# Loading w_in in quarters, and new placement rules for early copies, query scalings and middle groups, in a fused recurrent-attention and feed-forward kernel

## The chip, the cores and the metric

The kernel runs on one core of a Trainium2 chip. The metric is device time in microseconds (us) of one launch. Lower is better. All five engines of the core are used: TensorE (PE) for matmuls, VectorE (DVE), ScalarE (ACT), GpSimd (POOL), and SyncE (SP), which only issues transfers.

## The reference

Inputs are q, k, v and f_logit of shape 4 x 8 x 768 x 48 (batch, heads, time, width), and two weight matrices. The first half is a recurrence per batch and head, the second a two-layer feed-forward network over the 3072 tokens:

```python
f = 1.0 / (1.0 + np.exp(-f_logit))
for t in range(S):
    state = f[:, :, t, :, None] * state + np.einsum('bhd,bhe->bhde', k[:, :, t], v[:, :, t])
    y[:, :, t] = np.einsum('bhd,bhde->bhe', q[:, :, t], state)
# x = y with the heads side by side: 3072 tokens x 384
h = x @ w_in                                   # 384 x 2048
g = 0.5 * h * (1.0 + erf(h * inv_sqrt2))       # exact gelu
out = g @ w_out                                # 2048 x 384
```

## The kernel before

Time is cut into 24 chunks of 128 tokens, six for each of the four batches. Per chunk, the kernel loads f_logit, k, q and v (four transfers of 192 KB on SP's queue, lines 322 and 326). Exponentials on ACT (E and L for the gate, then RG and GT, lines 336 to 356) turn the recurrence into matmuls within the chunk. DVE scales keys (KP, line 359) and queries (QP, line 363); POOL casts the values (VC, line 369). PE transposes keys and queries (Tk, Tq, line 406), DVE and ACT copy them out of PSUM (KB, QT, lines 412 and 415), PE multiplies them (A, line 425), DVE masks the product (AM, line 429), PE multiplies by the values (Y, lines 477 and 481), and four copies (X and three x, lines 490 and 493) write the result, transposed, into a tile xT. The state passes from chunk to chunk through S (line 441), R (line 456), T (POOL, line 458) and SB (POOL, line 464).

The feed-forward part works on groups of chunks, whose sizes are `SIZES`. F1 (line 515) multiplies xT by w_in into PSUM, so it needs the x of every chunk of its group. GE (gelu on ACT, line 519) writes gT. F2 (line 532) multiplies gT by w_out in four steps r, of which step r needs the quarter r of w_out. A copy O (line 538) and a store on SP's queue follow. The exponentials and the gelu live in two different activation tables of ACT, and a change between them is a table load (line 604).

The weights are loaded from POOL's queue, because they are cast from float32 to bfloat16 on the way. Before, w_in comes in two column halves W0 and W1 of six transfers each (load_win, line 295), and w_out in four parts O0 to O3 (line 299). `ORDER` says in which order chunks (c0, c1, ...) and weights are wanted.

The order of all work is laid down ahead by a small planner (class Plan). Each operation is added with an engine, an assumed duration, what it reads and writes, and a priority. The planner places operations one after the other by the earliest start it computes, and among equal starts by the lower priority number. An operation with `alt` may go to a second engine; a copy that would go to ACT as an alternative is charged `BIAS` for it. Transfers are one serial resource of their own for the planner: a chunk's load counts 1.05, a half of w_in 1.2 or 0.4 per transfer, a part of w_out 2.4, and each is visible 2.0 after its end. The time that POOL spends on issuing a weight transfer is not in the plan. Afterwards the instructions are emitted in order of planned start, those that load weights `EARLY` = 1.5 ahead of it (line 601). Each engine and each queue then runs its own in that order.

Lines 592 to 612 add one more rule. If a weight's transfer started less than 3.0 ahead of a chunk's f_logit load in the plan, that load waits on the chip until a weight planned to start at least 2.5 ahead of it has landed:

```python
elif o.name.startswith("ldf") and ws and ws[-1][1] > o.start - 3.0:
    early = [w for w in ws if w[1] < o.start - 2.5]
    if early:
        gates[o.name] = early[-1][0]
```

Rings limit how far an engine can run ahead: xT has three buffers, gT two, the gelu's PSUM tiles three, the attention's PSUM tiles three. Idle matmuls (line 587) fill PE's planned gaps in the first 26 us.

Of the kernel before, what the change touches and what calls it, by code (L numbers as in the profile page):

```python
# [2 lines left out]

# [50 lines left out]

LAT = {"PE": 0.28, "ACT": 0.12, "DVE": 0.12, "POOL": 0.15, "DMA": 2.0}
SWITCH = 1.28
JITTER = 2.0


class Op:  # L60
    __slots__ = ("eng", "dur", "fn", "bufs", "prio", "deps", "table", "start", "end", "vis", "seq", "name", "alt", "nb")


class Plan:


    def __init__(self, seed=0, bias=0.0):
        self.ops, self.w, self.r = [], {}, {}
        self.rnd, self.bias = random.Random(seed) if seed else None, bias

    def add(self, eng, dur, fn, rd=(), wr=(), bufs=(), prio=0.0, deps=(), table=None, name="", alt=None):
        o = Op()
        o.alt, o.nb = alt, 0.0
        o.eng, o.dur, o.fn, o.bufs, o.prio, o.table, o.name = eng, dur, fn, tuple(bufs), prio, table, name
        o.start = o.end = o.vis = None
        o.seq = len(self.ops)
        d = list(deps)
        for k in rd:
            d += self.w.get(k, [])
        for k in wr:  # L80
            d += self.w.get(k, []) + self.r.get(k, [])
        for k in rd:
            self.r.setdefault(k, []).append(o)
        for k in wr:
            self.w[k] = [o]
# [12 lines left out]

    def run(self):
        free = {e: 0.0 for e in LAT}  # L100
        if self.rnd:
            for o in self.ops:
                o.prio += self.rnd.uniform(-JITTER, JITTER)
        act = None
        wait = {id(o): len(o.deps) for o in self.ops}
        after = {}
        for o in self.ops:
            for d in o.deps:
                after.setdefault(id(d), []).append(o)
        left = [o for o in self.ops if not o.deps]  # L110
        placed = []
        while left:
            best, stay, cand = None, None, []
            for o in left:
                ok = True
                t0 = o.nb
                for b in o.bufs:
                    v = b.ready()
                    if v is None:
                        ok = False  # L120
                        break
                    t0 = max(t0, v)
                if not ok:
                    continue
                for eng, dur in ((o.eng, o.dur),) if not o.alt else ((o.eng, o.dur), o.alt):
                    t = max(t0, free[eng])
                    for d in o.deps:
                        v = d.end if d.eng == eng and eng != "DMA" else d.vis
                        t = v if v > t else t
                    if o.table and o.table == act and (stay is None or t < stay):  # L130
                        stay = t
                    cand.append((t, o, eng, dur))
            for t, o, eng, dur in cand:
                if o.table and act and o.table != act and stay is not None and stay < t + 2 * SWITCH:
                    continue
                key = (int((t + (self.bias if o.alt and eng == "ACT" else 0)) * 20 + 0.999), o.prio, o.seq, t + dur)
                if best is None or key < best[0]:
                    best = (key, t, o, eng, dur)
            if best is None:
# [24 lines left out]
def kernel(  # L164
# [50 lines left out]
    P = Plan(SEED, BIAS)  # L215

    def copy(dst, src):
        if P.cur.eng == "ACT":
# [72 lines left out]

    def load_win(kk, half, ch):
        p0, p1, r0 = ((0, 96, 96 * kk), (96, 128, 288 + 32 * kk))[half]
        cs = slice(ch * d_ff // 2, (ch + 1) * d_ff // 2)
        return nc.gpsimd.dma_start(out=win[p0:p1, kk, cs], in_=moe_w_in[r0:r0 + p1 - p0, cs])

    def load_wout(j):
# [31 lines left out]
    def stage1(g):  # L329
# [13 lines left out]
        for n in ns:  # L343
# [16 lines left out]
                x["kp"].t()[:, :, 0:D], x["kt"].t(), rg.t(), ALU.mult),  # L360
                rd=[("rg", n), ("kt", n)] + [f"kpz{i}" for i in range(NQ)], wr=[("kp", n)],
                bufs=[x["kp"], x["kt"], rg], prio=pr, name=f"KP{n}")
            P.add("DVE", 0.57, lambda x=x, gt=gt: nc.vector.tensor_tensor(  # L363
                x["qp"].t()[:, :, 0:D], x["qt"].t(), gt.t(), ALU.mult),
                rd=[("gt", n), ("qt", n)] + [f"qpz{i}" for i in range(NQ)], wr=[("qp", n)],
                bufs=[x["qp"], x["qt"], gt], prio=pr + 1, name=f"QP{n}")

            def cast(x=x):
                nc.gpsimd.tensor_copy(x["vp"].t().rearrange("p (h x) -> p h x", x=VB)[:, :, 0:D], x["vt"].t())  # L369
# [23 lines left out]
    def attn(n):  # L393
# [17 lines left out]
        for hh in range(2):  # L411
            P.add("DVE", 0.42, lambda hh=hh: copy(
                kb.t()[64 * hh:64 * hh + D, :, hh, :], tps[0].t()[64 * hh:64 * hh + D]),
                rd=[("tk", n), "kbz0", "kbz1"], wr=[("kb", n, hh)], bufs=[tps[0], kb], prio=pr + 4, name=f"KB{n}", alt=("ACT", 0.6) if KBALT and n < ALTN else None)
        P.add("ACT", 0.6, lambda: copy(qT.t(), tps[1].t()),
              rd=[("tq", n)], wr=[("qT", n)], bufs=[tps[1], qT], prio=pr + 4, name=f"QT{n}", alt=("DVE", 0.42) if n < ALTN else None)
        ams = []
        for half in range(2):
            ap_, am = r_as.new(), r_am.new()
# [68 lines left out]
        def cols():  # L488
            return slice(j * C, (j + 1) * C)
        P.add("DVE", 0.55, lambda: copy(xT.t()[0:96, :, cols()], yp.t()[0:96, 0:3 * C].rearrange("p (a t) -> p a t", t=C)),  # L490
              rd=[("yp", n, 0), ("yp", n, 1)], wr=[("x", n, 3)], bufs=[yp, xT], prio=pr + 2, name=f"X{n}", alt=("ACT", 0.51) if n < ALTN else None)
        for kk in range(KO):
            P.add("DVE", 0.29, lambda kk=kk: copy(
                xT.t()[96:128, kk, cols()], yp.t()[32 * kk:32 * kk + 32, 3 * C:4 * C]),
                rd=[("yp", n, 1)], wr=[("x", n, kk)], bufs=[yp, xT], prio=pr + 2, name=f"x{n}", alt=("ACT", 0.3) if n < ALTN else None)

    def ffn_group(g):
        s, t = SIZES[g], G[g]
# [9 lines left out]
        for u in range(FO // pk):  # L508
            hps = r_hp.new()

            def f1(u=u, hps=hps):
                for i in range(pk):
                    fo = u * pk + i
                    for kk in range(KO):
                        nc.tensor.matmul(hps.t()[:, i * tok:(i + 1) * tok], win[:, kk, fo * 128:(fo + 1) * 128],  # L515
                                         xT.t()[:, kk, 0:tok], start=(kk == 0), stop=(kk == KO - 1))
# [8 lines left out]
        for s_, r in ([(s_, r) for r in range(4) for s_ in range(s)] if g < RMAJOR  # L525
# [10 lines left out]
            if r < 3:  # L536
                continue
            P.add("ACT", 0.49, lambda op=op, osb=osb: copy(osb.t(), op.t()[:, 0:d_model]),
                  rd=[("o", n)], wr=[("os", n)], bufs=[op, osb], prio=pr - 1000, name=f"O{n}", alt=("DVE", 0.55) if n < ALTN else None)
# [105 lines left out]
```

## Time and profile before

| what | value |
|---|---|
| median of 3 runs | 206.8 us (206.2 to 206.98) |
| the profiled execution | 207.0 us |
| its span, first to last instruction | 205.2 us |
| PE busy | 188.4 us (92%) |
| ACT busy | 135.7 us (66%) |
| DVE busy | 124.2 us (60%) |
| POOL busy | 54.5 us (27%) |
| TensorE clock granted | 0.992 of full speed |

A busy PE in the table is not a PE at its peak: matmuls overlap, and each record covers the whole passage of one. The share of useful work has to be counted from the number of matmuls in a stretch.

### The profile page before, as it was taken

Reading aid. Unit: us, or ns where it says so; the run is one execution under the profiler, and the core shown is the slowest. Engines: PE = TensorE matmul, PEld = TensorE weight load, DVE = VectorE, ACT = ScalarE, POOL = GpSimd, SP = SyncE. Lnnn points to the kernel's source line nnn. Section 1 sums busy time; section 2 is a strip of 40 time slices with the busy share of each in tenths; the row PEclk is TensorE's granted clock in tenths of the full one; section 3 lists DMA queues with packets and bytes.
Section 4 is the critical chain, followed back from the end, with each engine's and each line's share of the span. In section 5 each row is a group of like instructions: output and inputs, shape, how many; then the busy total and the mean of one; then the engine's idle time right before and its main releaser. Section 6 shows DMA issues by size and latency. Waiting matters only on the chain.

```text
span 205.2 us, 4574 instructions
## 1 busy us (share of the span) xinstructions
PE 188.4 (92%) x1735; PEld 127.7 (62%) x1746; DVE 124.2 (60%) x270; ACT 135.7 (66%) x247; POOL 54.5 (27%) x117
## 2 busy tenths in 40 slices
PE   6798769988889987997999999999999999999993
PEld 5797734556568666865665668655676655644551
DVE  6598750019793899999999579964189862000000
ACT  4445349954588677986977973887977773169510
POOL 7238990004023134422344032030032200000000
PEclk9799999999999999999999999999999999999999
DMA  7999999999999999998999999300121000220022
GB/s 125 189 171 161 183 168 159 191 181 239 205 206 186 188 227 192 167 203 192 202 189 175 190 202 221 86 0 2 42 77 38 3 0 0 80 77 0 0 77 77
DMA packets 106388, 27.02 MB, mean 132 GB/s; under 512 B 100480, under 2 KB 105600, under 8 KB 106368
## 3 DMA queue, kind: packets, MB, share of 16 engines
q1 hardware_dynamic: 103296, 23.60, 64.4%
q0 software_dynamic: 3072, 3.15, 10.1%
q8 instruction: 13, 0.21, 0.5%
q14 instruction: 7, 0.06, 0.1%
HBM read 25.17 MB, written 4.72 MB: 146 GB/s over the span
## 4 chain that ended last, share of the span: by engine, by line
PE 66%; DVE 10%; SPq 8%; DMA 7%; issue 4%; ACT 2%; POOL 1%; DVEq 0%; ACTq 0%; POOLq 0%
PE hps L532 26%; PE hps L515 24%; SPq L326 7%; PE aps L477 4%; DMA fl<-in_f_logit_dram 4%; PE tp L406 4%; PE aps L425 3%; DVE am L429 3%; DVE xT L221 2%; DMA vt<-in_v_dram 2%; PE aps L481 2%; PE aps L441 1%; DVE qp L363 1%; DMA out_dram<-osb 1%; DVE kp L359 1%
## 5 line engine op out<-in xcount | busy, mean ns | idle before, releaser
L515 PE MATMUL hps<-xT,win 128*128 128x512 bf16 (+1 forms) x325 | 68.0, 347 | 2.8 <-DVE xT L221 2.1
L532 PE MATMUL hps<-wout,gT 128*128 128x384 bf16 x384 | 68.2, 326 | 0.0
L519 ACT ACTIVATE gT<-hps 128x512 bf16<-128x512 f32 x96 | 56.4, 597 | 12.5 <-PE hps L515 8.3
L532 PEld LDWEIGHTS <-gT 128*128 128x128 bf16 x384 | 36.4, 98 | 21.9
L515 PEld LDWEIGHTS <-win 128*128 128x128 bf16 x336 | 31.5, 98 | 26.3 <-issue 3.5
L221 DVE CAST xT<-aps 96x384 bf16<-96x384 f32 (+1 forms) x92 | 32.7, 355 | 9.2 <-PE aps L481 6.0
L429 DVE TENSOR_TENSOR am<-aps,mask 128x512 bf16<-128x512 f32 x48 | 31.0, 685 | 6.8 <-PE aps L425 6.4
L369 POOL CAST vp<-vt 128x384 bf16<-128x384 f32 x24 | 12.7, 530 | 62.7 <-DMA vt<-in_v_dram 37.3
L477 PE MATMUL aps<-am,vp 128*128 128x128 bf16 x192 | 19.9, 219 | 3.0 <-DVE am L429 2.6
L458 POOL TENSOR_TENSOR tn<-rr,gl 128x384 f32<-128x384 f32 x16 | 13.2, 827 | 30.5 <-DVE rr L456 21.9
L359 DVE TENSOR_TENSOR kp<-kt,rg 128x384 bf16<-128x384 f32 x24 | 14.6, 609 | 11.0 <-ACT rg L356 10.7
L219 ACT ACTIVATE osb<-hps 128x384 f32<-128x384 f32 x18 | 8.8, 490 | 18.6 <-PE hps L532 18.4
L477 PEld LDWEIGHTS <-vp 128*128 128x128 bf16 x192 | 15.5, 98 | 8.5 <-issue 3.5
L464 POOL CAST sb<-tn 48x192 bf16<-48x192 f32 x40 | 16.0, 399 | 12.3 <-PE aps L477 3.9
L221 DVE COPY kb<-tp 48x512 bf16<-48x512 bf16 x42 | 17.5, 418 | 0.6
L336 ACT ACTIVATE fl<-fl 128x384 f32<-128x384 f32 (+2 forms) x15 | 10.7, 714 | 10.5 <-DMA fl<-in_f_logit_dram 10.4
L356 ACT ACTIVATE rg<-aps 128x384 f32<-128x384 f32 x24 | 11.8, 491 | 7.2 <-PE aps L349 6.1
L604 ACT ACT_TABLE_LOAD x12 | 15.4, 1283 | 0.9 <-PEq L629 0.7
L587 PE MATMUL hps<-trin 128*128 128x128 bf16 x170 | 14.0, 242 | 1.4 <-POOL trin L231 1.4
L425 PE MATMUL aps<-qT,kb 128*128 128x128 bf16 x192 | 15.0, 221 | 0.3 <-DVE qT L221 0.3
L481 PE MATMUL aps<-qT,sb 128*128 128x128 bf16 x80 | 15.1, 219 | 0.0
L219 ACT ACTIVATE qT<-tp 128x512 bf16<-128x512 bf16 x18 | 10.7, 596 | 6.5 <-PE tp L406 6.4
(42 smaller groups left out, 174.0 us busy)
## 6 DMA issues: line engine op xcount, KB each, us to landing
fl<-in_f_logit_dram SPq DMA_DIRECT2D x24, 192.0 KB, 4.5
kt<-in_k_dram SPq DMA_DIRECT2D x24, 192.0 KB, 4.6
qt<-in_q_dram SPq DMA_DIRECT2D x24, 192.0 KB, 4.5
vt<-in_v_dram SPq DMA_DIRECT2D x24, 192.0 KB, 4.5
out_dram<-osb SPq DMA_DIRECT2D x24, 192.0 KB, 1.9
wout<-in_moe_w_out_dram POOLq DMA_DIRECT2D x4, 384.0 KB, 7.9
win<-in_moe_w_in_dram POOLq DMA_DIRECT2D x6, 192.0 KB, 4.8
win<-in_moe_w_in_dram POOLq DMA_DIRECT2D x6, 64.0 KB, 4.3
```

Of the source, the lines that this page charges most:

```text
L219: nc.scalar.activation(dst, src, AF.Copy)
L221: nc.vector.tensor_copy(dst, src)
L359: P.add("DVE", 0.57, lambda x=x, rg=rg: nc.vector.tensor_tensor(x["kp"].t()[:, :, 0:D], x["kt"].t(), rg.t(), ALU.mult), rd=[("rg", n), ("k ...
L425: nc.tensor.matmul(ap_.t()[:, i * C:(i + 1) * C], kb.t()[:, p, hh, :], qT.t()[:, p, :], start=True, stop=True)
L429: P.add("DVE", 0.69, lambda ap_=ap_, am=am: nc.vector.tensor_tensor(am.t(), ap_.t().rearrange("p (h t) -> p h t", t=C), mask.unsqueeze(1). ...
L464: nc.gpsimd.tensor_copy(sb.t()[64 * hh:64 * hh + D, :, D * hh:D * hh + D], tn.t()[64 * hh:64 * hh + D, :, D * hh:D * hh + D])
L477: nc.tensor.matmul(yp.t()[:, p * C:(p + 1) * C], vwin(vp.t(), 2 * p + hh), ams[half].t()[:, 2 * (p % 2) + hh, :], start=(hh == 0), stop=(h ...
L481: nc.tensor.matmul(yp.t()[:, p * C:(p + 1) * C], osb.t()[:, p, :], qT.t()[:, p, :], start=False, stop=True)
L515: nc.tensor.matmul(hps.t()[:, i * tok:(i + 1) * tok], win[:, kk, fo * 128:(fo + 1) * 128], xT.t()[:, kk, 0:tok], start=(kk == 0), stop=(kk ...
L519: acts.append(P.add("ACT", 0.6, lambda u=u, hps=hps: nc.scalar.activation(view()[:, u * pk:(u + 1) * pk, :].rearrange("p a b -> p (a b)"), ...
L532: nc.tensor.matmul(op.t()[:, 0:d_model], view()[:, fo, s_ * C:(s_ + 1) * C], wout[:, fo, :], start=(fo == 0), stop=(fo == FO - 1))
L604: nc.scalar.preload_act_table_set("natural_log_exp_and_others" if table == "exp" else "gelu_and_others")
```

## The change

- w_in is loaded in four column quarters (`NW = 4`), six transfers each, so 24 instead of 12. F1 waits for the quarter that it reads.
- `ORDER` is now c0 to c3, then W0 to W3, then c4, then O0 to O3. Before, O3 came ahead of W0, O1 ahead of c4, and O0 and O2 behind it.
- `SIZES` goes from 4,2,2,4,4,4,4 to 4,2,2,1,2,1,4,4,4. The exponentials' batches end in 4,4 instead of 4,2,1,1.
- Alternatives: QP of the first six chunks may go to POOL (`QALTN = 6`). KB may no longer go to ACT (`KBALT = 0`). QT, X, x and O may change engine for four chunks instead of six (`ALTN`). The charge for leaving the home engine is 0.4 instead of 0.8 and holds in every direction. The planner, which is run twice, remembers the home engine.
- Fixed offsets are added to the priorities by kind of operation (`PRI`). The unused random offsets are removed.
- `LOCK` is 4 instead of 12: rules that tie an exponentials' batch to a gelu hold from chunk 4 on.

```diff
-        o.eng, o.dur, o.fn, o.bufs, o.prio, o.table, o.name = eng, dur, fn, tuple(bufs), prio, table, name
+        o.eng, o.dur, o.fn, o.bufs, o.prio, o.table, o.name = eng, dur, fn, tuple(bufs), prio + self.pri.get(name.rstrip("0123456789."), 0), table, name
...
-                for eng, dur in ((o.eng, o.dur),) if not o.alt else ((o.eng, o.dur), o.alt):
+                for eng, dur in ((o.home, o.dur),) + (o.alt or ()):
...
-                key = (int((t + (self.bias if o.alt and eng == "ACT" else 0)) * 20 + 0.999), o.prio, o.seq, t + dur)
+                key = (int((t + (self.bias if eng != o.home else 0)) * 20 + 0.999), o.prio, o.seq, t + dur)
...
-    SIZES = [4, 2, 2, 4, 4, 4, 4]
-    ORDER = ['c0', 'c1', 'c2', 'c3', 'O3', 'W0', 'W1', 'O1', 'c4', 'O0', 'O2']
+    SIZES = [4, 2, 2, 1, 2, 1, 4, 4, 4]
+    ORDER = ['c0', 'c1', 'c2', 'c3', 'W0', 'W1', 'W2', 'W3', 'c4', 'O0', 'O1', 'O2', 'O3']
     EARLY = 1.5
+    NW = 4
...
-    LOCK = 12
-    KBALT = 1
-    ALTN = 6
-    BIAS = 0.8
-    SEED = 0
+    LOCK = 4
+    KBALT = 0
+    ALTN = 4
+    BIAS = 0.4
+    PRI = {'VC': 5, 'E': 1, 'KP': 10, 'X': -2, 'QT': 20, 'x': -1, 'Y': 2, 'SB': -1, 'A': 1, 'S': 2}
+    QALTN = 6
...
-    BATCH = [1, 1, 1, 1, 1, 1, 2, 2, 2, 2, 2, 4, 2, 1, 1]
+    BATCH = [1, 1, 1, 1, 1, 1, 2, 2, 2, 2, 2, 4, 4]
...
+    def eng():
+        return nc.vector if P.cur.eng == "DVE" else nc.gpsimd
...
-        cs = slice(ch * d_ff // 2, (ch + 1) * d_ff // 2)
+        cs = slice(ch * d_ff // NW, (ch + 1) * d_ff // NW)
...
-            P.add("DVE", 0.57, lambda x=x, gt=gt: nc.vector.tensor_tensor(
+            P.add("DVE", 0.57, lambda x=x, gt=gt: eng().tensor_tensor(
                 x["qp"].t()[:, :, 0:D], x["qt"].t(), gt.t(), ALU.mult),
...
-                bufs=[x["qp"], x["qt"], gt], prio=pr + 1, name=f"QP{n}")
+                bufs=[x["qp"], x["qt"], gt], prio=pr + 1, name=f"QP{n}",
+                  alt=(("POOL", 0.9),) if n < QALTN else None)
...
-            P.add("PE", 0.645 + 0.0025 * (3 * pk - 3), f1, rd=[("x", n, i) for n in ns for i in range(4)] + [f"win{u * pk // 8}"],
+            P.add("PE", 0.645 + 0.0025 * (3 * pk - 3), f1, rd=[("x", n, i) for n in ns for i in range(4)] + [f"win{u * pk * NW // FO}"],
...
-            P.w[f"win{ch}"] = [P.add("DMA", (1.2, 0.4)[half], lambda kk=kk, half=half, ch=ch: load_win(kk, half, ch),
+            P.w[f"win{ch}"] = [P.add("DMA", (2.4, 0.8)[half] / NW, lambda kk=kk, half=half, ch=ch: load_win(kk, half, ch),
```

More of the change, by code (lines that the diff above doesn't have):

```diff
@@ L1 @@
-import random
 from contextlib import ExitStack
@@ L56, with __init__ @@
 SWITCH = 1.28
-JITTER = 2.0
 class Op:
-    __slots__ = ("eng", "dur", "fn", "bufs", "prio", "deps", "table", "start", "end", "vis", "seq", "name", "alt", "nb")
+    __slots__ = ("eng", "dur", "fn", "bufs", "prio", "deps", "table", "start", "end", "vis", "seq", "name", "alt", "nb", "home")
 class Plan:
-    def __init__(self, seed=0, bias=0.0):
+    def __init__(self, pri, bias):
         self.ops, self.w, self.r = [], {}, {}
-        self.rnd, self.bias = random.Random(seed) if seed else None, bias
+        self.pri, self.bias = pri, bias
     def add(self, eng, dur, fn, rd=(), wr=(), bufs=(), prio=0.0, deps=(), table=None, name="", alt=None):
         o = Op()
-        o.alt, o.nb = alt, 0.0
-        o.eng, o.dur, o.fn, o.bufs, o.prio, o.table, o.name = eng, dur, fn, tuple(bufs), prio, table, name
+        o.alt, o.nb, o.home = alt, 0.0, eng
+        o.eng, o.dur, o.fn, o.bufs, o.prio, o.table, o.name = eng, dur, fn, tuple(bufs), prio + self.pri.get(name.rstrip("0123456789."), 0), table, name
         o.start = o.end = o.vis = None
@@ L100, in run @@
         free = {e: 0.0 for e in LAT}
-        if self.rnd:
-            for o in self.ops:
-                o.prio += self.rnd.uniform(-JITTER, JITTER)
         act = None
@@ L213 @@
     tpp = ctx.enter_context(tc.tile_pool(name="tpp", bufs=2, space=PSUM))
-    P = Plan(SEED, BIAS)
+    P = Plan(PRI, BIAS)
+    def eng():
+        return nc.vector if P.cur.eng == "DVE" else nc.gpsimd
     def copy(dst, src):
@@ L413, in attn @@
                 kb.t()[64 * hh:64 * hh + D, :, hh, :], tps[0].t()[64 * hh:64 * hh + D]),
-                rd=[("tk", n), "kbz0", "kbz1"], wr=[("kb", n, hh)], bufs=[tps[0], kb], prio=pr + 4, name=f"KB{n}", alt=("ACT", 0.6) if KBALT and n < ALTN else None)
+                rd=[("tk", n), "kbz0", "kbz1"], wr=[("kb", n, hh)], bufs=[tps[0], kb], prio=pr + 4, name=f"KB{n}", alt=(("ACT", 0.6),) if KBALT and n < ALTN else None)
         P.add("ACT", 0.6, lambda: copy(qT.t(), tps[1].t()),
-              rd=[("tq", n)], wr=[("qT", n)], bufs=[tps[1], qT], prio=pr + 4, name=f"QT{n}", alt=("DVE", 0.42) if n < ALTN else None)
+              rd=[("tq", n)], wr=[("qT", n)], bufs=[tps[1], qT], prio=pr + 4, name=f"QT{n}", alt=(("DVE", 0.42),) if n < ALTN else None)
         ams = []
@@ L490, in attn @@
         P.add("DVE", 0.55, lambda: copy(xT.t()[0:96, :, cols()], yp.t()[0:96, 0:3 * C].rearrange("p (a t) -> p a t", t=C)),
-              rd=[("yp", n, 0), ("yp", n, 1)], wr=[("x", n, 3)], bufs=[yp, xT], prio=pr + 2, name=f"X{n}", alt=("ACT", 0.51) if n < ALTN else None)
+              rd=[("yp", n, 0), ("yp", n, 1)], wr=[("x", n, 3)], bufs=[yp, xT], prio=pr + 2, name=f"X{n}", alt=(("ACT", 0.51),) if n < ALTN else None)
         for kk in range(KO):
@@ L494, in attn @@
                 xT.t()[96:128, kk, cols()], yp.t()[32 * kk:32 * kk + 32, 3 * C:4 * C]),
-                rd=[("yp", n, 1)], wr=[("x", n, kk)], bufs=[yp, xT], prio=pr + 2, name=f"x{n}", alt=("ACT", 0.3) if n < ALTN else None)
+                rd=[("yp", n, 1)], wr=[("x", n, kk)], bufs=[yp, xT], prio=pr + 2, name=f"x{n}", alt=(("ACT", 0.3),) if n < ALTN else None)
     def ffn_group(g):
@@ L538, in ffn_group @@
             P.add("ACT", 0.49, lambda op=op, osb=osb: copy(osb.t(), op.t()[:, 0:d_model]),
-                  rd=[("o", n)], wr=[("os", n)], bufs=[op, osb], prio=pr - 1000, name=f"O{n}", alt=("DVE", 0.55) if n < ALTN else None)
+                  rd=[("o", n)], wr=[("os", n)], bufs=[op, osb], prio=pr - 1000, name=f"O{n}", alt=(("DVE", 0.55),) if n < ALTN else None)
             P.add("DMA", 0.6, lambda n=n, osb=osb: nc.sync.dma_start(out=out[n * C:(n + 1) * C, :], in_=osb.t()),
```

## The prediction

> **What bounds the kernel now.** I first asked where PE, busy for 92% of the span, does no useful work. The counts of matmuls by line, priced at the pace of unbroken runs in the chain (43 of 512 columns in 9.44, 64 of w_out in 10.41, eight of 128 in 0.45), give 7.1 us of useful work in 0 to 29, 10.7 of 11 in 29 to 40, 13.6 of 18 in 40 to 58, 31.7 of 39 in 58 to 97, 30.9 of 33 in 97 to 130. So about 22 us go before F1 starts, 4.4 in 40 to 58, 7.3 in 58 to 97; from 97 on a floor of some 6% (2.1 of 33) is lost. The same 6% of 39 is 2.5, so 58 to 97 holds 4.8 that could be had back.
>
> The second view is the page's rows of 40 slices (5.1 us each), with two of its groups:
>
> ```profile
> DVE  6598750019793899999999579964189862000000
> POOL 7238990004023134422344032030032200000000
> DMA  7999999999999999998999999300121000220022
> L369 POOL CAST vp<-vt 128x384 bf16<-128x384 f32 x24 | 12.7, 530 | 62.7 <-DMA vt<-in_v_dram 37.3
> L604 ACT ACT_TABLE_LOAD x12 | 15.4, 1283 | 0.9 <-PEq L629 0.7
> ```
>
> POOL, nearly idle elsewhere, is full in slices 4 and 5, transfers are full up to about 128, and DVE is full again from 70 to 112. Third, POOL in order of time (start, us, idle before):
>
> ```profile
> 17.16 0.93 POOL L299 DMA_DIRECT2D wout<-in_moe_w_out_dram  x1
> 18.09 0.55 POOL L295 DMA_DIRECT2D win<-in_moe_w_in_dram  x1
> 18.66 0.83 POOL L458 TENSOR_TENSOR tn<-rr,gl 128x384 f32<-128x384 f32 x1
> ...
> 21.62 0.71 POOL L369 CAST vp<-vt 128x384 bf16<-128x384 f32 x1
> 22.28 1.99 POOL L295 DMA_DIRECT2D win<-in_moe_w_in_dram  x4
> ...
> 28.27 2.29 POOL L299 DMA_DIRECT2D wout<-in_moe_w_out_dram  x3
> 43.69 0.50 POOL L369 CAST vp<-vt 128x384 bf16<-128x384 f32 x1 [13.13 <-DMA vt<-in_v_dram]
> 48.13 0.51 POOL L369 CAST vp<-vt 128x384 bf16<-128x384 f32 x1 [3.93 <-DMA vt<-in_v_dram]
> ```
>
> Issuing one w_in transfer takes POOL 0.5 whatever its size; POOL works without a gap from 17.2 to 30.6. All three remaining w_out parts are out before VC4, which waits for chunk 4's values until 43.69. Fourth, SP's own waits, SP in order of time, and PE where F1 of the groups 0 and 1 starts:
>
> ```profile
> SPq L322 <- DMA win<-in_moe_w_in_dram: 15.4, 1, 15.4
> ```
> ```profile
> 32.10 0.37 SPq L322 DMA_DIRECT2D fl<-in_f_logit_dram  x1
> ```
> ```profile
> 29.02 10.52 PE L515 MATMUL hps<-xT,win 128*128 128x512 bf16 x47 [1.26 <-DVE xT L221]
> 39.38 3.41 PE L532 MATMUL hps<-wout,gT 128*128 128x384 bf16 x20
> 57.66 1.24 PE L515 MATMUL hps<-xT,win 128*128 128x256 bf16 x6 [0.47 <-DVE xT L221]
> ```
>
> The one gated load is chunk 4's f_logit: 15.4 of wait for w_in, and everything behind it on SP waits too. F1 of group 0 waits for x of chunk 3, not for w_in; F1 of group 1 waits for x of chunk 5.
>
> **What the Trainium skill says.** "DMA: Bandwidth & Descriptors", "Anatomy of one DMA — SWDGE (gpsimd) path": a wait before a transfer is held by the issuing sequencer, not by the DMA engines. The trace agrees: SP stood 15.4 and issued nothing. "GPSIMD Engine Reference", "4.1 Engine selection": an elementwise operation of two inputs is about twice as slow on GpSimd. Here 827 ns (line 458) against 552 to 593 on DVE, 1.4 to 1.5 times. "SBUF — State Buffer", "SBUF: two separate sides": DVE with two SBUF inputs and a GpSimd operation that reads SBUF exclude each other. QP3 at 21.27 took 0.70 beside VC3's 0.71 (usually 0.55 and 0.50), which agrees. "ScalarE: Activation LUTs", "What ACT_TABLE_LOAD costs": 1283 ns and a drain of 1380. The trace has the 1283, but the next activation follows the load at 40.20 after 0.01; I use 1.28.
>
> **The change, part by part.**
>
> *w_in in quarters.* Twelve more issues on POOL: 12 x 0.51 = 6.1 us. They fall where POOL is full. Up to VC2 nothing changes, so the 18th issue (the end of W2) comes at 17.1 + 18 x 0.51 + T2 0.8 + SB2 1.0 + VC3 0.7 + T3 0.8 + SB3 0.8 = 30.4, with one QP on POOL (0.83) 31.2, less 1.6 if T3 and SB3 fall behind it. Landing takes 4.3 to 4.8 (transfers' rows of the page, 192 and 64 KB): 34 to 36; I take 35. The last w_in issue is at 34, its landing at 38. F1 of group 0 has 10.5 us of work; it may start 0 to 4 earlier (DVE gets relief, below), but its last quarter cannot start before 38 and takes 2.6: end at 40.6, against 39.5. So the quarters gain nothing for F1. The half-as-long pieces may slow the transfers: not at all, or at worst to the rate of a chunk's loads, which are of the same 768 KB in far smaller pieces and came 4.2 apart (casts at 7.17 and 11.37). POOL's pace (six issues 3.1, with the work between them 4.3) covers even that.
>
> *The new order.* The planner's own costs tell the order, not the time. c0 to c3 end at 16 x 1.05 = 16.8, W3 at 16.8 + 9.6 = 26.4, c4 at 30.6, O0 starts there, O1 at 33.0, O2 at 35.4, O3 at 37.8. VC4 is ready at 30.6 + 2.0 = 32.6, on a POOL that is free in the plan. O2 is emitted at 35.4 - 1.5 = 33.9, O3 at 36.3. So VC4 now stands ahead of O2 and O3 on POOL, and they cannot be issued until the values of chunk 4 have landed. Before, VC4 was ready at 37.4 and the last O emitted at 36.3. The gates change as well: c4's load waits for the last transfer of W2 (planned 23.8, under 26.4 - 2.5), c5's load (planned 40.2) for O2 (35.4).
>
> That is a chain: W2 lands at 35; c4's four loads take from 6.3 (0.74 to the cast at 7.17, an uncrowded queue) to 11.5 (32.10 to 43.69 here); 8 is taken, so 43. VC4 0.5; O2 issued 43.5 to 44.3; it lands 5 to 7.9 later (7.9 is the page's median for w_out in a crowd; by then little else moves), 49.5, O3 at 51. Then c5's loads, 6.3: 56, against 48.1. F2 of chunk 0 runs its steps r = 0 and 1 near 42 to 44 and stands until 49.5 for r = 2. What stands behind it on PE are its own 14 steps (14 x 0.65 = 9.1) and A4, Y4. x5 followed the cast VC5 of 48.13 by 9.5; from 56, and with 7.6 to 9.5, it comes at 63.6 to 65.5. F1 of group 1 then starts near 64 instead of 57.7: **+6.4**, with ends of +2 (W2 at 34, c4 in 6.3, O2 in 5, x5 in 7.6: 59.5) and +10.
>
> *Placement of early copies, QP on POOL.* DVE sheds up to 6 x 0.59 of QP, six QT at 0.42 (the charge now falls on QT's move to DVE) and takes back six KB at 0.42 from ACT: 3.5 us less, all in chunks 0 to 5. This shortens the way to x3, worth 0 to 4 us alone, but F1's end is held by W3 as shown: 0 taken. A QP3 that sits on POOL among the w_in issues would come at about 23 instead of 21.3, which is also covered until 38. In chunks 4 and 5 the shorter DVE work is the lower end of 7.6 used above.
>
> *Smaller middle groups.* PE's columns are the same: 128-column matmuls run at 0.056 each (eight in 0.45), 256-column ones at 0.109 (30 in 3.27), so no group size costs PE anything that the trace shows. Gelu stays at 96 activations. What they bring: F1 need not wait for four, or two, chunks' x. F1 of chunks 8 to 11 started at 97.3 only when x11 was there; now F1 of chunk 8 can fill PE before. Of the 4.8 to be had in 58 to 97 I take 3; the bounds are 0 and 4.8. **-3**.
>
> *Table loads.* Twelve now, one pair per alternation. Two more groups can cost up to four more, 4 x 1.28 = 5.1 us of ACT. ACT is busy for 31.0 of 39 us in 58 to 97, so half might reach PE. The planner avoids a switch where work of the same table is near, so 0 is taken; 0 to 2.6.
>
> *Offsets, LOCK, the last batches.* The new tie of chunks 6 and 7's exponentials to group 0's last gelu holds at a time (41) when those chunks are not loaded; the last batch of four instead of 2,1,1 lies at 130 and later, where PE has a backlog: 0, with -1 to +1.
>
> Sum on the profiled execution: span 205.2 + 6.4 - 3 = 208.6, and 1.8 around it (207.0 - 205.2): 210.4. The median of the runs lies 0.2 below that execution: 210.2. Part of the delay may be absorbed, since PE had stood again at 74 to 80 for chunks 6 and 7 whatever happened before; I take 0.7 for it: **209.5**.
>
> **The rivals.** 0.5% of 206.8, about 1.0 us, is what a measurement can tell from no change.
>
> (a) *The transfers' chain is covered and the middle wins.* If c4 is back by 41 and O2 lands by 46, F1 of group 1 is late by 2 or less, and DVE's 3.5 us are felt in x5. Then -4.8 and +2 or 0: 202 to 204, best guess 203.5. For it: the stalls in 58 to 97 are real, and DVE was full there. Against it: POOL's issue time is measured and the order is arithmetic. It decides at a delay of about 4 in F1 of group 1. Chance 0.28.
>
> (b) *They cancel*: late by 4 to 5, middle back by 4 to 5, 206 to 207.8. Chance 0.15. It includes that the quarters do nothing since x3 holds F1.
>
> (c) *ACT becomes the bound in the middle*: four more table loads, no gain from the groups, the full delay: 205.2 + 6.4 + 2.6 + 1.6 = 215.8; with half of each 212.5. Against it: ACT idles a fifth there. Chance 0.09.
>
> The forecast itself, 207.8 to 212, has 0.48.
>
> **How the numbers follow.** Slower is the forecast and (c), 0.57; same (b), 0.15; faster (a), 0.28. The likeliest is 209.5, its own range 207.8 to 212. The range that leaves out two tenths runs from 203.3 (about half of (a) below it) to 212.5 (the worse half of (c) above it).
>
> **What would show it.** F1 of group 0 ends near 40.6 with a stand before its last quarter. On POOL two w_out issues come after VC4, at 43 to 45. SP waits for wout at c5. DMA has a hole in slices 9 and 10. F2 stands 4 or more us near 45, and F1 of group 1 starts at 62 or later. After that PE loses under 5 in the 39 us that follow. Wrong: O2 issued before VC4; W2 landed by 32; F1 of group 1 before 60; more than 14 table loads.

## The result, and the profile after

| | before | changed |
|---|---|---|
| median | 206.73 us | 212.63 us (211.57 to 213.34) |
| ratio, 95% interval | | 1.0285 (1.0231 to 1.0339) |
| profiled execution, its span | 207.0, 205.2 | 212.11, 210.1 |
| F1 of group 0: start, end | 29.0, 39.5 | 32.0, 47.1 |
| start of F1 of group 1 | 57.7 | 62.6 |
| from there to the end | 147.5 | 147.5 |
| table loads | 12 | 16 |

The kernel became slower, as forecast, but by 5.9 us instead of 2.8, and its time lies 0.13 above the stated range, which is less than the spread of its own runs. The two rows ahead of the last already divide it: all of the 4.9 us of span are lost before F1 of group 1 starts, and nothing is won afterwards. Of the kernels timed further below, one (e_halves_both) was profiled in a slower execution at a lower clock than most of its runs, so its profile is read only up to the start of F1 of group 1.

The rows of the page that answer to those shown of before (40 slices of 5.25 us; PEclk is the granted TensorE clock in tenths):

```profile
DVE  6589450002958286879989998947789771000000
POOL 7259994030603404312303543213041200000000
PEclk9999669699999997999999999999999999999999
DMA  7999789969999989999999999900111000220022
...
L605 ACT ACT_TABLE_LOAD x16 | 20.5, 1283 | 1.0 <-PEq L630 0.7
```

POOL is now full from 15.8 to 31.5, in three slices instead of two. The transfers have holes in the same stretch and from 42.0 to 47.3. The clock falls to 0.6 from 21.0 to 31.5 and again from 36.8 to 42.0, where the kernel before had full speed. POOL in order of time (start, us, idle before):

```profile
16.65 2.74 POOL L295 DMA_DIRECT2D win<-in_moe_w_in_dram  x5
19.39 0.86 POOL L459 TENSOR_TENSOR tn<-rr,gl 128x384 f32<-128x384 f32 x1
...
23.35 0.50 POOL L370 CAST vp<-vt 128x384 bf16<-128x384 f32 x1
23.80 4.44 POOL L295 DMA_DIRECT2D win<-in_moe_w_in_dram  x9
...
32.16 1.55 POOL L299 DMA_DIRECT2D wout<-in_moe_w_out_dram  x2
42.45 0.50 POOL L370 CAST vp<-vt 128x384 bf16<-128x384 f32 x1 [8.74 <-DMA vt<-in_v_dram]
42.90 1.49 POOL L299 DMA_DIRECT2D wout<-in_moe_w_out_dram  x2
```

This is the block that was forecast: O2 and O3 leave only after the cast of chunk 4 at 42.45. But the cast of chunk 3, at 21.62 before, is also late, at 23.35. SP's own waits show the two gates, for w_in at c4 and now for w_out at c5 too:

```profile
SPq L322 <- DMA win<-in_moe_w_in_dram: 13.7, 1, 13.7
SPq L322 <- DMA wout<-in_moe_w_out_dram: 13.7, 1, 13.7
```

PE where F1 of the groups 0 and 1 and the third step of F2 start, and ACT ahead of the first gelu, both in order of time:

```profile
32.04 0.38 PE L516 MATMUL hps<-xT,win 128*128 128x512 bf16 x1 [0.94 <-ACT xT L219]
...
37.04 10.09 PE L516 MATMUL hps<-xT,win 128*128 128x512 bf16 x39 [1.51 <-ACT gT L520]
...
49.80 2.11 PE L533 MATMUL hps<-wout,gT 128*128 128x384 bf16 x12 [0.72 <-DMA wout<-in_moe_w_out_dram]
...
62.60 2.13 PE L516 MATMUL hps<-xT,win 128*128 128x256 bf16 x18
```
```profile
34.00 0.52 ACT L336 ACTIVATE fl<-fl 128x384 f32<-128x384 f32 x1 [1.72 <-DMA fl<-in_f_logit_dram]
34.56 0.52 ACT L339 ACTIVATE lf<-fl 128x384 bf16<-128x384 f32 x1
35.10 1.28 ACT L605 ACT_TABLE_LOAD   x1
36.39 1.57 ACT L520 ACTIVATE gT<-hps 128x512 bf16<-128x512 f32 x3
```

This was not forecast. The exponentials of chunk 4 now stand ahead of the first gelu on ACT. They wait for chunk 4's f_logit until 34.00, the table follows, and the first gelu runs at 36.39 although its PSUM tile was full near 33. F1 fills its three PSUM tiles and stands until 37. Its other 39 matmuls take 10.09, in part at half the clock (0.50 in 38 to 40). So F1 of group 0 ends at 47, and O2's landing at 49.8 costs only 0.72. From 37.04 to 62.60 that is PE's only stand of 0.2 us or more.

### The profile page after: what moved, and what is told of

It reads as the page before. It is cut to its first block, busy times and chain, and to the rows that moved or that the text cites. A ratio compares the mean times of both kernels' runs of the same rounds, so it can differ in the third digit from the quotient of the medians.

```text
span 210.1 us, 4778 instructions
## 1 busy us (share of the span) xinstructions
PE 192.5 (92%) x1846; PEld 136.6 (65%) x1846; DVE 120.2 (57%) x262; ACT 141.9 (68%) x251; POOL 61.0 (29%) x131
## 4 chain that ended last, share of the span: by engine, by line
PE 71%; DMA 11%; SPq 6%; POOL 5%; DVE 2%; issue 2%; ACT 1%; POOLq 0%; ACTq 0%; DVEq 0%
PE hps L533 28%; PE hps L516 25%; DMA vt<-in_v_dram 7%; SPq L326 4%; PE aps L426 4%; PE aps L478 4%; PE tp L407 4%; POOL win L295 4%; DMA wout<-in_moe_w_out_dram 3%; PE aps L482 2%; PE aps L349 2%; DMA win<-in_moe_w_in_dram 1%; SPq L322 1%; PE aps L442 1%; POOL vp L370 1%
## 5 line engine op out<-in xcount | busy, mean ns | idle before, releaser
L516 PE MATMUL hps<-xT,win 128*128 128x512 bf16 (+2 forms) x432 | 70.7, 314 | 2.7 <-ACT gT L520 1.5
L533 PE MATMUL hps<-wout,gT 128*128 128x384 bf16 x384 | 69.6, 326 | 0.7 <-DMA wout<-in_moe_w_out_dram 0.7
L516 PEld LDWEIGHTS <-win 128*128 128x128 bf16 x432 | 38.2, 99 | 26.0 <-issue 4.2
L370 POOL CAST vp<-vt 128x384 bf16<-128x384 f32 x24 | 12.7, 528 | 52.7 <-DMA vt<-in_v_dram 28.7
L219 ACT ACTIVATE osb<-hps 128x384 f32<-128x384 f32 x24 | 11.8, 490 | 22.3 <-PE hps L533 21.9
L221 DVE COPY kb<-tp 48x512 bf16<-48x512 bf16 x48 | 20.1, 418 | 3.8 <-PE tp L407 3.0
L219 ACT ACTIVATE qT<-tp 128x512 bf16<-128x512 bf16 x24 | 14.3, 594 | 8.9 <-PE tp L407 8.8
L465 POOL CAST sb<-tn 48x192 bf16<-48x192 f32 x40 | 14.6, 364 | 16.3 <-PE aps L482 9.7
L426 PE MATMUL aps<-qT,kb 128*128 128x128 bf16 x192 | 17.3, 227 | 0.2 <-DVE kb L221 0.2
L588 PE MATMUL hps<-trin 128*128 128x128 bf16 x174 | 15.7, 254 | 1.4 <-POOL trin L231 1.4
L426 PEld LDWEIGHTS <-kb 128*128 128x128 bf16 x192 | 13.9, 102 | 3.6 <-DVE kb L221 0.4
```

The lines of the kernel that those rows point to most:

```text
L219: nc.scalar.activation(dst, src, AF.Copy)
L221: nc.vector.tensor_copy(dst, src)
L426: nc.tensor.matmul(ap_.t()[:, i * C:(i + 1) * C], kb.t()[:, p, hh, :], qT.t()[:, p, :], start=True, stop=True)
L533: nc.tensor.matmul(op.t()[:, 0:d_model], view()[:, fo, s_ * C:(s_ + 1) * C], wout[:, fo, :], start=(fo == 0), stop=(fo == FO - 1))
L588: nc.tensor.matmul(buf.t()[:, 0:C], trin, trin, start=True, stop=True)
```

## The experiments

Twelve more kernels were timed against the kernel before. "Rest" is the span's end less the start of F1 of group 1, from each kernel's profiled execution. The first row repeats the change.

| kernel | median | ratio (95%) | F1 of group 1 | rest |
|---|---|---|---|---|
| the change | 212.63 | 1.0285 (1.0231 to 1.0339) | 62.6 | 147.5 |
| a_vc4_late | 209.21 | 1.0159 (1.0120 to 1.0199) | 61.9 | 145.7 |
| a_e4_late | 211.81 | 1.0273 (1.0192 to 1.0354) | 65.0 | 145.4 |
| a_vc4_e4_late | 208.27 | 1.0123 (1.0047 to 1.0199) | 60.0 | 145.8 |
| a_all_three | 209.65 | 1.0181 (1.0139 to 1.0223) | 62.2 | 145.9 |
| b_halves | 212.24 | 1.0271 (1.0201 to 1.0341) | 64.2 | 145.1 |
| b_old_order | 213.75 | 1.0342 (1.0282 to 1.0403) | 62.6 | 148.5 |
| b_old_groups | 216.24 | 1.0432 (1.0353 to 1.0510) | 64.5 | 150.8 |
| d_order_halves | 208.33 | 1.0091 (1.0064 to 1.0117) | 59.0 | 148.6 |
| e_halves_both | 205.59 | 0.9947 (0.9929 to 0.9965) | 58.5 | (not read) |
| c_new_groups | 205.37 | 0.9951 (0.9926 to 0.9976) | 57.4 | 146.2 |
| c_only_transfers | 220.26 | 1.0675 (1.0614 to 1.0737) | 63.9 | 153.2 |
| d_no_placement | 207.62 | 1.0061 (1.0039 to 1.0082) | 56.5 | 149.3 |

F1 of group 1 also moves between executions: the changed kernel and b_old_groups have the same plan up to there and show 62.6 and 64.5, since in the latter chunk 4's f_logit reached ACT at 35.77 instead of 34.00. So a difference of 1 or 2 us between two single profiles means little by itself; the medians and ratios carry the verdicts.

### Which of two delays: chunk 4's cast on POOL, or its exponentials on ACT

The first three kernels keep the change's plan and alter only the order of emission, by giving single operations another place in the sorted list.

```diff
+    when = {o.name: o.start for o in P.placed}
+    put = {}
+    put["VC4"] = when["wout3"] - EARLY + 0.01                  # a_vc4_late, a_vc4_e4_late, a_all_three
+    put.update({m: when["GE0.15"] + 0.001 * (i + 1)
+                for i, m in enumerate(["E4", "L4", "C4", "GM4"])})  # a_e4_late, a_vc4_e4_late, a_all_three
+    put["VC3"] = when["T2"] + 0.01                             # a_all_three
-    for o in sorted(P.placed, key=lambda o: (o.start - ...
+    for o in sorted(P.placed, key=lambda o: (put.get(o.name, o.start) - ...
```

> The changed kernel with one order altered: the cast of chunk 4's values stands behind the last two w_out issues on POOL, so that these no longer wait for chunk 4. Theory 1 (the prediction's: the transfers' chain from c4 over O2 to c5 sets the start of F1 of group 1): O2 and O3 are issued at 34 and land by 42, c5 is loaded some 7 us earlier, F1 of group 1 starts at 58 to 59 instead of 62.6, and 3.5 to 4.5 us are gained, 208 to 209. Theory 2 (F1 of group 0 itself is late, it ends at 47 instead of 39.5, and the chain is covered by that): only the stand of 0.7 before the third step of F2 goes, and x5 comes a little earlier; 0.5 to 1.5 us, 211 to 212.

> The changed kernel with the exponentials of chunk 4 (E4, L4 on ACT, C4 and its sums on PE) put behind the last gelu of group 0, where the kernel before had them. The first gelu no longer waits for chunk 4's f_logit. Both theories: F1 of group 0 ends 3 to 4.6 us earlier, near 43. Theory 1: the start of F1 of group 1 stays, since O2 still lands at 49.8: gain 0 to 1. Theory 2, if it alone were true: the gain reaches the end, 3 to 4.5 us, 208 to 209. If two delays of nearly equal length stand side by side, this run gains 0 to 1 and so does the one with the cast moved.

> The changed kernel with both orders altered: the cast of chunk 4 behind the w_out issues, and the exponentials of chunk 4 behind the last gelu of group 0. Theory 1: no more than with the cast alone. Two delays side by side: F1 of group 0 ends near 43, F2 follows without a stand, F1 of group 1 starts at 58 to 59, gain 3.5 to 4.5 us where each alone gives about 1: 208 to 209.

The cast alone brought 2.6 us of the 5.9 (1.0285 to 1.0159). The exponentials alone brought nothing that can be told (1.0273), both together came to 1.0123. Theory 1 gets most of its time but not its place: F1 of group 1 starts only 0.7 earlier, as theory 2 had it, and 1.8 come after it. PE of a_vc4_late:

```profile
37.21 10.12 PE L516 MATMUL hps<-xT,win 128*128 128x512 bf16 x39 [1.51 <-ACT gT L520]
...
61.90 2.13 PE L516 MATMUL hps<-xT,win 128*128 128x256 bf16 x18
```

Between these two lines PE has no stand of 0.2 us or more. So with O2 and O3 out of the way the lateness of F1 of group 0 alone still puts F1 of group 1 at 61.9, 4.2 later than in the kernel before. The stand for O2 adds 0.7 in the changed kernel.

What comes after: in the changed kernel PE stands 2.4 at 80 for the exponentials of chunks 10 and 11, whose f_logit is late:

```profile
80.56 0.32 PE L349 MATMUL aps<-lf,trin 128*128 128x384 bf16 x1 [1.64 <-ACT lf L339]
...
81.81 0.48 PE L349 MATMUL aps<-lf,trin 128*128 128x384 bf16 x1 [0.75 <-ACT gt L352]
```

The clock then is 0.50 in 82 to 84. In a_vc4_late the stands there come to 1.2 and the clock stays up. So the transfers' delay is felt again some 20 us later. Why the exponentials alone bring nothing is seen in PE of a_e4_late. F1 of group 0 now runs through and ends at 42.4, but F2 stands three times before 50:

```profile
32.07 10.30 PE L516 MATMUL hps<-xT,win 128*128 128x512 bf16 x46 [0.24 <-DVE xT L221]
...
45.45 0.32 PE L349 MATMUL aps<-lf,trin 128*128 128x384 bf16 x1 [2.42 <-ACT lf L339]
...
48.30 1.44 PE L533 MATMUL hps<-wout,gT 128*128 128x384 bf16 x4 [1.78 <-DMA wout<-in_moe_w_out_dram]
50.23 4.00 PE L533 MATMUL hps<-wout,gT 128*128 128x384 bf16 x12 [0.48 <-DMA wout<-in_moe_w_out_dram]
```

The first stand, 2.42, is the edit's own: put after the last gelu, chunk 4's exponentials, with a table load ahead of them, hold up its sums, which stand in PE's order ahead of F2's second step. So the edit moves one wait rather than removing it, and the same stand of 2.42 is in a_vc4_e4_late. The other two, 1.78 and 0.48, are for O2 and O3; in a_vc4_e4_late, where w_out leaves in time, they are gone and F2 runs on from 45.71. In a_e4_late the stands cost more than their length: the last 12 matmuls shown take 4.00 and the four ahead of them 1.44, where the changed kernel has 2.11 for 12 and 0.81 for four. The granted clock was 0.50 from 48 to 54, which makes 2.5 us for these 16. Stands and clock together eat up the 4.7 us by which F1 of group 0 ended earlier. The pair's 1.0123 can't be told from the cast's 1.0159.

### Taking the late cast of chunk 3 out as well

> The changed kernel with three orders altered: as the last, and the cast of chunk 3's values stands before the later w_in issues (behind T2). It then runs at 20.5 instead of 23.35, PE no longer stands 2.15 before S3, the granted clock does not fall near 24 to 31, and F1 of group 0 starts at 29.5 to 30 instead of 32.0. Two delays side by side plus the late x3: another 1 to 2 us, 206.5 to 208, about level with the kernel before. If the late x3 does not matter since w_in's last quarter holds F1: the same as the last run.

The step itself did what was expected: the cast ran at 20.28, F1 of group 0 started at 28.6, and the clock stayed up (1.00 in 22 to 30). All of it was lost again, and the run is not faster than the one without it. PE of a_all_three:

```profile
28.59 0.38 PE L516 MATMUL hps<-xT,win 128*128 128x512 bf16 x1 [0.94 <-ACT xT L219]
...
40.60 0.82 PE L533 MATMUL hps<-wout,gT 128*128 128x384 bf16 x4 [1.09 <-DMA wout<-in_moe_w_out_dram]
43.33 0.81 PE L533 MATMUL hps<-wout,gT 128*128 128x384 bf16 x4 [0.34 <-DMA wout<-in_moe_w_out_dram]
45.30 1.44 PE L533 MATMUL hps<-wout,gT 128*128 128x384 bf16 x4 [1.16 <-DMA wout<-in_moe_w_out_dram]
47.35 4.00 PE L533 MATMUL hps<-wout,gT 128*128 128x384 bf16 x12 [0.61 <-DMA wout<-in_moe_w_out_dram]
```

F2 now waits four times for the next part of w_out, 3.2 us in all, and the clock is at half again (0.50 in 46 to 50), so that the last two lines take 5.44 instead of 2.92. With 24 w_in issues ahead of it, w_out leaves POOL only from 32.66 on. That is a third delay: w_out behind the quarters. It was covered as long as F1 of group 0 was late.

### The quarters or the order

These three and the next keep the rest of the change and are planned anew.

```diff
-    ORDER = ['c0', 'c1', 'c2', 'c3', 'W0', 'W1', 'W2', 'W3', 'c4', 'O0', 'O1', 'O2', 'O3']
-    NW = 4
+    ORDER = ['c0', 'c1', 'c2', 'c3', 'W0', 'W1', 'c4', 'O0', 'O1', 'O2', 'O3']   # b_halves
+    NW = 2                                                                      # b_halves, d_order_halves
+    ORDER = ['c0', 'c1', 'c2', 'c3', 'O3', 'W0', 'W1', 'W2', 'W3', 'O1', 'c4', 'O0', 'O2']  # b_old_order
+    ORDER = ['c0', 'c1', 'c2', 'c3', 'O3', 'W0', 'W1', 'O1', 'c4', 'O0', 'O2']   # d_order_halves
```

> The changed kernel with w_in in two halves again (12 transfers instead of 24) and everything else of the change kept: its order of transfers, groups, placements. The order on POOL is the same, chunk 4's cast still stands ahead of two w_out issues. Tells the cost of the twelve further issues from that of the order. If the issues matter (the chain starts later by them): chunk 3's cast runs near 21.5 instead of 23.35, F1 of group 0 starts near 29.5 instead of 32.0, O0 and O1 are out at 27 instead of 33.7, F1 of group 1 starts 1 to 3 us earlier than at 62.6; 210 to 211.5. If the order alone matters: within 0.7 of the changed kernel, 212 to 213.

> The changed kernel with the order of transfers of the kernel before (O3 ahead of w_in, O1 ahead of c4, O0 and O2 behind it), but w_in still in quarters. Chunk 4's cast comes behind the last w_out issue by the plan itself, its exponentials behind group 0's last gelu, and c4's load waits for all of w_in. If the order is the main cause: F2 of group 0 has no stand for O2, F1 of group 1 starts at 58 to 60, 207 to 209. If the further issues are the main cause: 211 or more.

> The changed kernel with the order of transfers of the kernel before and w_in in halves again; what is left of the change are the smaller middle groups, the placements, the priority offsets. If the transfers' part of the change carries the whole loss: F1 of group 1 starts at 57 to 58.5 as before, the middle gives 1.5 to 2, and the kernel is faster than the one before, 204.5 to 206. If the placements or offsets cost something early on: 206.5 to 208.

Neither undone alone helps: 1.0271 with halves in the new order, 1.0342 with quarters in the old order, against 1.0285. Undone together they leave 1.0091, above both ranges that were expected. The two single runs seem to contradict each other: by its expectation b_halves says that the order alone matters, b_old_order that the further issues do. Both hold, since each part makes the full delay by itself, on different ways. The clock is not the cause of the whole loss either: b_old_order was profiled at a mean of 1.000 and lost as much.

With halves in the new order, POOL is relieved as expected (chunk 3's cast at 21.30, F1 at 28.7, w_out at 26.94), but now two parts of w_out are issued ahead of c4's loads. Chunk 4's f_logit is issued at 28.77 and used at 36.47, 7.7 later, against 3.7 in the changed kernel, and ACT stands much longer with the first gelu behind it. ACT of b_halves:

```profile
36.47 0.52 ACT L336 ACTIVATE fl<-fl 128x384 f32<-128x384 f32 x1 [7.55 <-DMA fl<-in_f_logit_dram]
```

F1 of group 0, which had started at 28.7, filled its three tiles and went on at 39.5. With quarters in the old order there is no such block. Instead the last w_out issues slip from 29.66 (d_order_halves) to 33.87, c4's gate from a wait of 16.8 to one of 19.6, its cast from 44.80 to 48.19. F2 stands 2.80 for w_out, and F1 of group 1 starts at 62.6 instead of 59.0. Here twelve more issues of 0.5 on POOL cost 2.5% of the time (1.0342 against 1.0091, 5.4 us of medians).

> The changed kernel with w_in in two halves, chunk 4's cast behind the last w_out issue and chunk 4's exponentials behind group 0's last gelu: all three things that the runs so far show to delay F1 of group 1 are taken out, groups and placements of the change are kept. If these are the whole of the loss: F1 of group 0 runs 28.7 to 39.3 without a stand, O2 and O3 are issued by 30, F1 of group 1 starts at 56.5 to 58, then 145.7 to the end: 204 to 206, level with or faster than the kernel before. If the loads of c5 stay behind (their gate still waits for O2): F1 of group 1 at 59 to 60 and 206.5 to 208.

The edit is NW = 2 with b_halves' order, and the cast's and exponentials' places of a_vc4_e4_late. With all three taken out, this kernel is slightly faster than the one before: 0.9947 (0.9929 to 0.9965). F1 of group 0 runs without a stand (29.10, 47 recorded matmuls in 10.30), all four w_out issues leave at 26.76, F1 of group 1 starts at 58.5. The stand of 2.42 for chunk 4's sums is still there. So the three together carry the loss: the cast's place, the exponentials' place, and the number of w_in issues. What each is worth is not shown. Alone, moving the cast gave 2.6 us, and neither moving the exponentials nor going back to halves gave anything that can be told; with halves only the pair of moves was tried. The kernel is also no better than the smaller groups alone (c_new_groups below, 0.9951), so the new order and the placements win nothing that can be told even here.

### The groups, the transfers and the placements apart

b_old_groups is the change with the old groups; c_new_groups is the kernel before with the new ones; c_only_transfers is the kernel before with the quarters and the new order.

```diff
-    SIZES = [4, 2, 2, 1, 2, 1, 4, 4, 4]                     # b_old_groups; c_new_groups the other way
-    BATCH = [1, 1, 1, 1, 1, 1, 2, 2, 2, 2, 2, 4, 4]
-    LOCK = 4
+    SIZES = [4, 2, 2, 4, 4, 4, 4]
+    BATCH = [1, 1, 1, 1, 1, 1, 2, 2, 2, 2, 2, 4, 2, 1, 1]
+    LOCK = 12
```

> The changed kernel with the groups, the exponentials' batches and LOCK of the kernel before (4,2,2,4,4,4,4); all up to chunk 7 is as in the changed kernel. If the smaller middle groups gain what the traces suggest (145.7 us from the start of F1 of group 1 to the end where transfers are not late, against 147.5 before): 1 to 3 us slower than the changed kernel, 213.5 to 215.5. If the four further table loads eat the gain: within 0.7 of it. If they cost more: 211 or less.

> The kernel before with the smaller middle groups, the batches ending in 4,4 and LOCK 4, nothing else of the change. If the groups gain 2 to 3.6 us whatever comes ahead of them: 203 to 205. If their gain in the changed kernel came only because its transfers are late: 206 to 207.5. If they cost table loads that matter without the late start: 208 or more.

> The kernel before with the transfers' part of the change alone: w_in in quarters, c4 ahead of all of w_out. If this part carries the loss: F1 of group 1 starts at 62 to 64 instead of 57.7, the end 4.5 to 6.5 later, 211 to 213. If the placements are needed for it: 208 or less.

The groups gain in both surroundings: 3.6 us where the transfers are late (216.24 to 212.63, rest 150.8 to 147.5), a little more than expected, and 0.5% (0.9951, 0.9926 to 0.9976; about 1.0 us) where they are not, less than the 2 to 3.6 expected. The transfers' part alone costs far more than expected, 6.75%. It delays the first gelu too (F1 of group 0 goes on at 38.09), so the order of transfers is enough for that block. F1 of group 1 starts 6.2 later, within what was expected, and the rest grows by another 5.7. The chunks 8 to 11 come late, and F1 of the group of four that they form needs the last of them. F1 of that group in the kernel before, and in c_only_transfers:

```profile
97.34 0.59 PE L515 MATMUL hps<-xT,win 128*128 128x512 bf16 x2
```
```profile
109.58 0.40 PE L426 MATMUL aps<-qT,kb 128*128 128x128 bf16 x4 [0.77 <-DVE xT L222]
109.82 2.11 PE L516 MATMUL hps<-xT,win 128*128 128x512 bf16 x9
```

That is 12.5 later, and from there to the end both kernels take nearly the same, 107.9 and 107.3. PE's clock was also at 0.50 from 98 to 108 in c_only_transfers, with DVE busy for 9.63 of these 10 us; how much of the 5.7 comes from the late loads and how much from the clock was not parted. Here the small groups were worth most where something ahead of them was late.

```diff
-    KBALT = 0          # d_no_placement: on top of d_order_halves
-    ALTN = 4
-    BIAS = 0.4
-    QALTN = 6
+    KBALT = 1
+    ALTN = 6
+    BIAS = 0.8
+    QALTN = 0
```

> The kernel with the old order of transfers and w_in in halves (208.3), with the placements of the kernel before as well (no QP on POOL, copies shared for six chunks with the old charge). What is left of the change are the groups, the priority offsets and the planner's memory of the home engine. The groups alone measured 205.4. If the placements cost the 3.0 between the two: 205 to 206. If the offsets cost them, by the order of the middle: 207.5 to 209, with PE's useful work in 97 to 130 again near 28.4 of 33 instead of 31.

It came to 1.0061, beside 1.0091 with the placements and 0.9951 for the groups alone; the intervals of the first two overlap. So the placements cost at most a few tenths of a per cent in the old order, and most of the 1.4% between 1.0091 and 0.9951 is with what is still left: the offsets, or the planner's memory of the home engine, which were not parted. F1 of group 1 starts even earlier (56.5); the time is lost later, for instance in 97 to 130, where PE's useful work, counted as in the prediction, is 28.9 of 33 us against 31.1 with the groups alone. e_halves_both has the same offsets and memory and is level with the groups alone, so it is this plan that is slower and not the offsets in any plan.

## Why the prediction was wrong

The sign and the block on POOL were right; the size was not. The step that failed is the time after F1 of group 1 starts. It was forecast 3.7 us shorter (-3 for the groups, -0.7 absorbed) and stayed at 147.5. The way to the start of F1 of group 1 was wrong too, though its number came near. By the prediction's own steps:

- **The chain c4, O2, c5.** Forecast: c4's values 43, O2 49.5, c5's values 56, F1 of group 1 at 64. Measured: 42.45, 49.8, 55.2, 62.6. Two errors cancelled in it. W2 landed at 30.35, not 35: T3 and SB3 fell behind it, and the small pieces landed 3.1 to 3.4 after their issue, not 4.3 to 4.8. And c4 took 12.1 instead of 8, with w_in's last quarter and two parts of w_out beside it; with all four parts beside it, in a_vc4_late, it took 16.6. x5 came 7.1 after the cast, a little under the lower end used. The term was +6.4; it measured +4.9. That this is near is in part luck: F2's stand for O2 cost 0.7 and not 4 or more. And a_vc4_late shows that 4.2 come by the next step, even when F2 does not wait for w_out and c5's f_logit is issued at 43.69 instead of 47.73. Whether the chain alone would have given as much is not shown, since a_e4_late (65.0) brings a stand of its own.
- **"Its last quarter cannot start before 38 and takes 2.6: end at 40.6."** This failed. F1 of group 0 ended at 47. The late chunk 3 was noted and taken as covered, but F1 started at 32.0 (at 30.4 in b_old_groups, where the clock stayed up), and the exponentials of chunk 4, planned now ahead of the first gelu, were not seen at all. The prediction followed POOL's and SP's queues past the moved c4, and left out ACT's. It also has no term for the clock: at half speed in part, F1's last 39 matmuls took 10.09, and 8.58 at full speed in c_only_transfers, which is 1.5 of the 4.2. Without this lateness the forecast path is there: in a_e4_late F1 ends 4.7 earlier and F2 stands 2.26 for O2 and O3.
- **"Smaller middle groups: -3" and "Part of the delay may be absorbed: 0.7."** The groups measured 3.6 in the changed kernel (b_old_groups), but only 1.0 in the kernel before (c_new_groups), from whose stalls the 3 was worked out. So the 3 comes near for another reason than the one given: the groups soften a delay. The 0.7 failed: with the old groups the time after F1 of group 1 is 150.8 against 147.5, so the delay was not absorbed but added 3.3, which the groups then took back. That reading rests on one profile each. c_only_transfers, which has neither offsets nor placements, points the same way with 153.2, but what the offsets and placements do in the new order was not tried apart. The sum with what was measured is 205.2 + 4.9 + 0 = 210.1, in place of 205.2 + 6.4 - 3.7 = 207.9.
- **"Table loads: 0."** There are 16, the most that was allowed for. The groups gain with them; what the loads cost by themselves was not measured.
- **"QP on POOL, placements: 0."** Consistent with d_no_placement against d_order_halves, in the old order. Of the offsets, put at 0 with -1 to +1, all that is known is that they and the memory of the home engine together go with a loss of about 2 in the old order.
- **Rival (a)** decided at a delay of 4 in F1 of group 1; it was 4.9, and even without it the groups would have gained 1.0, not 4.8. **Rival (c)** gave 212.5, which is close to what was measured, but its mechanism did not come about: it had no gain from the groups, and they gained 3.6.
- **The signs.** Two w_out issues after the cast (42.9 to 44.4), a gate on w_out at c5, and F1 of group 1 after 62 came. The hole in the transfers came earlier (42 to 47) than the slices named. The stand of 4 us for O2 near 45 did not come (0.72), nor did the low loss in the 39 us after F1 of group 1: by the same count of matmuls it is about 7, where the kernel before has 7.3 in its own 39 us. Two of the four signs of being wrong came true, W2 landing by 32 (30.35) and more than 14 table loads (16).

What stays open: how the offsets and the memory of the home engine share the loss in the old order, what each of the three delays is worth by itself, and how much of the 2.6 us of a_vc4_late comes from c5 itself and how much from the second stand at 80.

## What to carry to other kernels

When a load is moved, follow every operation that consumes it on every in-order queue that it now overtakes: here one cast on POOL, one exponential on ACT and one gate on SP, each harmless in a plan that assumes punctual transfers, and each of them stood for the late chunk with the urgent work of others behind it. Where several such delays cover one another, undoing one can show little or nothing; take them out together before calling one innocent. Look at the granted clock beside every stand of PE, since the stand can cost more than its length. And a transfer issued by POOL has a price on POOL: twelve more cost 6 us of a queue that also carried the critical casts.

## What the runs showed of the hardware that was not expected

The granted clock often fell to half beside a stand of PE that is short, but not always. All engines in 22 to 30, in the kernel before, the changed one and b_old_groups (busy us of PE, PE's weight loads, DVE, ACT and POOL, then the clock, the transfers' share, GB/s):

```profile
22.00:30.00 8.00, 5.66 (x80) 4.75 (x81) 5.33 (x11) 3.30 (x7) 7.94 (x16) 1.00 1.04 170
```
```profile
22.00:30.00 8.00, 6.09 (x60) 6.09 (x60) 3.55 (x9) 0.53 (x2) 7.89 (x17) 0.57 0.79 109
```
```profile
22.00:30.00 8.00, 4.81 (x76) 4.27 (x76) 4.69 (x10) 0.53 (x2) 7.89 (x17) 1.00 0.79 107
```

The last two have the same plan up to there, and PE stands for the late cast of chunk 3 in both:

```profile
23.91 0.48 PE L442 MATMUL aps<-vp,kp 128*128 128x96 bf16 x4 [2.15 <-POOL vp L370]
```
```profile
23.98 0.33 PE L442 MATMUL aps<-vp,kp 128*128 128x96 bf16 x4 [2.12 <-POOL vp L370]
```

Only the changed kernel lost its clock there. The same stand, 2.00 to 2.17, came with half the clock in a_vc4_late, a_e4_late and a_vc4_e4_late. After a stand of 2.42 the clock fell in a_e4_late, where one of 1.78 followed, and not in a_vc4_e4_late; after one of 2.80 in b_old_order it stayed at 1.00. The Trainium skill, "TensorE: Matmul & The Clock Gate", "What's actually happening", gives half the clock after an idle window of about 3.4 us. The half agrees (0.50 at the lowest); the stands here were shorter, and their length alone does not tell which of them halve the clock. What does stays open.

What half the clock costs is seen in runs of equal count: 12 matmuls of F2 in 4.00 (a_e4_late) instead of 2.11 (the changed kernel), and 39 of F1 in 10.09 (the changed kernel) instead of 8.58. The latter in c_only_transfers:

```profile
38.09 8.58 PE L516 MATMUL hps<-xT,win 128*128 128x512 bf16 x39 [1.51 <-ACT gT L520]
```

Pieces of w_in of half the length landed no later after their issue: 3.4 for 96 KB, against 4.8 for 192 KB before. The transfers were also less crowded then (109 against 170 GB/s in 22 to 30), so the two do not compare the pieces alone.
